# Scores and the K remainder of gate/up in 32-row TensorE tiles, two head groups alternating

## The chip, the cores and the metric

The kernel runs on one core of one Trainium2 chip. The metric is device time in microseconds (us), the median of the runs shown. TensorE does the matmuls, VectorE (DVE) and ScalarE (ACT) read their results from PSUM, GpSimd (POOL) masks, and SyncE (SP) issues most DMAs. All times here are in us unless marked ns.

## The reference

A transformer block with attention and a gated MLP side by side on the same normalized input. S = 2048 tokens, D = 576, 32 heads of 18, a causal window of 256 keys, F = 4608, all tensors bf16.

```python
xn  = layernorm(x)
q, k, v = split_heads(xn @ wqkv)                 # 32 heads x 18
p   = softmax(where(0 <= i - j < 256, q @ k.T * 18**-0.5, -1e9))
att = merge_heads(p @ v) @ wo
h   = silu(xn @ w1) * (xn @ w3)                  # 576 -> 4608
out = x + att + h @ w2                           # 4608 -> 576
```

## The kernel before

The program is a list of operations, each with its engine and the buffers it reads (`r`), writes (`w`) or writes further (`j`). From these `_Prog.resolve` works out the semaphore waits. Each engine runs its operations in the order of the list, so the order in the code is the schedule: an operation that waits holds up all that stands behind it on its engine.

The tokens are worked in four chunks of 512 (`c`), and each chunk has two stages.

The first stage loops over 36 units (`u`), each 128 columns of F. `unit_full` does up (`w3`) and gate (`w1`), four matmuls each with 128 rows of K. D = 576 leaves 64 rows, which `unit_rest` does as two matmuls on 64-row tiles of the array: one for up in rows 0 to 63, one for gate in rows 64 to 127. `unit_act` reads the up bank on VectorE (`us`, L541) and the gate bank on ScalarE (`th`, L543). `unit_h` makes `gs` (L549, which reads the gate bank again) and `hT` (L552) on VectorE.

Attention is laid between the units. A group `g` is four heads, a step `s` one key block of 128 against up to 384 queries; chunk 0 has three steps per group, later chunks four. Steps 1 and 2 have one part, steps 0 and 3 two parts of 128 and 256 columns. `scores` (L433) works on 64-row tiles, two heads to a tile with the other head's query rows zero, and writes four PSUM banks, the SBK banks. `exps` (L447) reads them in two pairs, `p` = 0 and 1. `masks` (L459) runs on GpSimd. Two units after a group's last step `pv` (L475) multiplies by v on four column tiles into the bank UB, `pv_out` copies it to `uT` (L484), and a unit later `heads_back` (L489) transposes it back and `heads_out` normalizes it into `oall`.

The next chunk's layer norm is also laid into the units: `ln_stats`, two units later `ln_apply` (L307), two later `xn_trans` (L317) through UB.

The second stage multiplies `hT` by W2 (`p2_item`, L584) and `oall` by `wo` into the SBK banks. Every eighth item it takes one tile of the next chunk's q, k or v projection (`qk_tile`, `v_half`) or, at four items, `o_trans`. `repack` (L385) moves q and k from `stage` into head layout by DMA, in chunk 0 on SP's queue, later on ScalarE's.

PSUM has eight banks: a ring of three (RB) for units and projections, four SBK, one UB. A unit takes two ring banks. In each iteration the order is

```python
unit_full(c, u); unit_rest(c, u)
scores(c, *step); pv(...); heads_back(...)
unit_act(u); exps(c, *step); unit_h(u)
pv_out(...); heads_out(...); masks(c, *step); ln_stats / ln_apply / xn_trans
```

The gate/up weights come in fills of 512 columns of F (`load_w13`, five DMAs each, three buffers), the remainder's weights among them (`wr`).

Of the kernel before, what the change touches and what calls it, by code (L numbers as in the profile page):

```python
# [162 lines left out]
def bass_parallel_sum__sliding_block__glu_gated_swiglu__prompt_kernel(  # L163
# [32 lines left out]
    with ExitStack() as es:  # L196
# [7 lines left out]
        xn = [sb(f"xn{i}", [128, D]) for i in range(2)]  # L204
# [5 lines left out]
        xnT = sb("xnT", [128, 2, 5, CH])  # L210
# [4 lines left out]
        wr = [sb(f"wr_{i}", [128, 512]) for i in range(NW13)]  # L215
# [3 lines left out]
        qk = sb("qk", [128, 4, G, CH])  # L219
        va = sb("va", [128, 2 * TB, G, 4 * VW])  # L220
        pt = sb("pt", [128, NPT, 2, 384])
        uT = [sb(f"uT{i}", [128, CH]) for i in range(2)]
# [9 lines left out]
        RB = es.enter_context(nc.psum_tensor("rb", [128, 3, 512], dt.float32))  # L232
        SBK = es.enter_context(nc.psum_tensor("sbk", [128, 4, 512], dt.float32))
        UB = es.enter_context(nc.psum_tensor("ub", [128, 512], dt.float32))
        UBH = UB[:, :].bitcast(dt.bfloat16)
        UT4 = UBH[:, 0:512].rearrange("p (t h c) -> p t h c", t=TB, h=4)

        ring_ctr = 0

        def ring():  # L240
            nonlocal ring_ctr
            i = ring_ctr % 3
            ring_ctr += 1
            return i

# [18 lines left out]
        def load_w13():  # L264
            nonlocal nfill
            if nfill >= NC * NFC:
                return
            s = nfill % NW13
            c0 = (nfill % NFC) * 512
            nfill += 1  # L270
            k = [("w13", s)]
            d = f"w13_{s}"
            add("sp", lambda e: e.dma_start(
                w3[s][:, 0:3, :], B_w3[0:384, c0:c0 + 512].rearrange("(kd p) f -> p kd f", p=128)), w=k, dma=d)
            add("sp", lambda e: e.dma_start(w3[s][:, 3, :], B_w3[448:576, c0:c0 + 512]), j=k, dma=d)
            add("sp", lambda e: e.dma_start(
                w1[s][:], B_w1[0:512, c0:c0 + 512].rearrange("(kd p) f -> p kd f", p=128)), j=k, dma=d)
            add("sp", lambda e: e.dma_start(wr[s][0:64, :], B_w3[384:448, c0:c0 + 512]), j=k, dma=d)
            add("sp", lambda e: e.dma_start(wr[s][64:128, :], B_w1[512:576, c0:c0 + 512]), j=k, dma=d)
# [25 lines left out]
        def ln_apply(t, s):  # L305
            i = t % 2
            add("dve", lambda e: e.tensor_scalar(  # L307
                xn[i][:], xp[s][:], mv[i][:, 0:1], rstd[i][:, 0:1], op0=ALU.subtract, op1=ALU.mult),
                r=[("xp", s), ("mv", i), ("rstd", i)], w=[("xn", i)])

        def xn_trans(t, bank, key, evac):
            i = t % 2
            c, tt = divmod(t, TB)
            bv = bank.rearrange("p (k f) -> p k f", f=128)
            for kd in range(5):
                k0 = min(kd * 128, D - 128)
                add("pe", lambda e, kd=kd, k0=k0: e.transpose(bv[:, kd, :], xn[i][:, k0:k0 + 128], ident[:]),  # L317
                    r=[("xn", i), "ident"], **{"w" if kd == 0 else "j": [key]})
            dst = xnT[:, c % 2, :, tt * 128:(tt + 1) * 128]
            if evac == "dve":  # L320
                add("dve", lambda e: e.tensor_copy(dst, bv[:, 0:5, :]), r=[key], w=[("xnT", c % 2, tt)])
            else:
                add("act", lambda e: e.activation(dst, bv[:, 0:5, :], ACT.Copy), r=[key], w=[("xnT", c % 2, tt)])
# [5 lines left out]
        def qk_tile(c, i):  # L329
# [6 lines left out]
            add("dve", lambda e: e.tensor_copy(stage[:, i, :], RB[:, b, :]), r=[("rb", b)], w=[("st", i)])  # L336
# [34 lines left out]
        def repack(c, g, eng):  # L371

            kq, kk = ("q", g), ("k", g, c % 2)
            first = True
            for hh in range(4):
                a, b = hh % 2, 2 + c % 2
                for tq, tk, rq, rk, o, n in pieces(Dh * (4 * g + hh)):
                    p0 = 32 * hh + o
                    if tq != tk:
                        moves = [(qk[p0:p0 + n, a:b + 1:b - a, g, :], stage[rq:rq + n, tq:tk + 1:tk - tq, :])]  # L380
                    else:
                        moves = [(qk[p0:p0 + n, a, g, :], stage[rq:rq + n, tq, :]),
                                 (qk[p0:p0 + n, b, g, :], stage[rk:rk + n, tk, :])]
                    for dst, src in moves:
                        add(eng, lambda e, dst=dst, src=src: e.dma_start(dst, src),  # L385
                            r=[("st", tq), ("st", tk)], dma=f"qk{g}", **{"w" if first else "j": [kq, kk]})
# [38 lines left out]
        def scores(c, g, s):  # L425
            for p in range(2):
                for r in range(2):
                    bk = 2 * p + r
                    first = True
                    for kb, qb, nq, col in parts(c, s):  # L430
                        kc, kt = divmod(kb, TB)
                        qo = (qb - c * TB) * 128
                        add("pe", lambda e, p=p, r=r, bk=bk, kc=kc, kt=kt, qo=qo, nq=nq, col=col: e.matmul(  # L433
                            SBK[:, bk, col:col + 128 * nq],
                            qk[64 * r:64 * r + 64, 2 + kc % 2, g, kt * 128:(kt + 1) * 128],
                            qk[64 * r:64 * r + 64, p, g, qo:qo + 128 * nq],
                            start=True, stop=True, tile_position=(64 * r, 0)),
                            r=[("k", g, kc % 2), ("q", g)], **{"w" if first else "j": [("sb", bk)]})
                        first = False

        def exps(c, g, s):
            nonlocal pt_ctr
            for p in range(2):
                sl = pt_ctr % NPT
# [3 lines left out]
                    pt[:, sl, :, :], SBK[:, 2 * p:2 * p + 2, 0:384], ACT.Exp, scale=scale),  # L448
                    r=[("sb", 2 * p), ("sb", 2 * p + 1)], w=[("pt", sl)])

        def masks(c, g, s):
            for p in range(2):
                sl = pt_of[(c, g, s, p)]
                v = pt[:, sl, :, :].rearrange("p h (b q) -> p h b q", q=128)
                key = [("pt", sl)]
# [10 lines left out]

        def pv(c, g):

            seq = [(s, part) for s in steps_of(c) for part in parts(c, s)]
            for n, (s, (kb, qb, nq, col)) in enumerate(seq):  # L470
                qo = (qb - c * TB) * 128
                for hh in range(4):
                    sl = pt_of[(c, g, s, hh % 2)]
                    slot = kb % (2 * TB)
                    add("pe", lambda e, hh=hh, sl=sl, slot=slot, qo=qo, nq=nq, col=col, n=n: e.matmul(  # L475
                        UB[32 * hh:32 * hh + VW, qo:qo + 128 * nq],
                        va[:, slot, g, VW * hh:VW * (hh + 1)],
                        pt[:, sl, hh // 2, col:col + 128 * nq],
                        start=(n == 0), stop=(n == len(seq) - 1), tile_position=(0, 32 * hh), skip_group_check=True),
                        r=[("pt", sl), ("va", slot)], **{"w" if n == 0 and hh == 0 else "j": ["ub"]})  # L480

        def pv_out(g):
            i = g % 2
            add("dve", lambda e: e.tensor_copy(uT[i][:], UB[:, :]), r=["ub"], w=[("uT", i)])  # L484

        def heads_back(g):
            i = g % 2
            for tt in range(TB):
                add("pe", lambda e, tt=tt: e.transpose(  # L489
                    UBH[:, tt * 128:(tt + 1) * 128], uT[i][:, tt * 128:(tt + 1) * 128], ident[:]),  # L490
                    r=[("uT", i), "ident"], **{"w" if tt == 0 else "j": ["ub"]})

        def heads_out(g):
            i = g % 2
            add("dve", lambda e: e.reciprocal(rden[i][:], UT4[:, :, :, Dh]), r=["ub"], w=[("rden", i)])
            ov = oall[:, :, g * 72:(g + 1) * 72].rearrange("p t (h d) -> p t h d", d=Dh)
            add("dve", lambda e: e.tensor_tensor(
                ov, UT4[:, :, :, 0:Dh], rden[i][:].unsqueeze(3).to_broadcast([128, TB, 4, Dh]), ALU.mult),
                r=["ub", ("rden", i)], w=[("o", g)])
# [16 lines left out]
        def unit_full(c, u):  # L516
            fc, fl = divmod(u, 4)
            sl = (c * NFC + fc) % NW13
            bu, bg = ring(), ring()
            unit_banks[u] = (bu, bg)  # L520
            for b, ws, blocks in ((bu, w3, (0, 1, 2, 4)), (bg, w1, (0, 1, 2, 3))):
                for kd in range(4):
                    add("pe", lambda e, kd=kd, b=b, ws=ws, xb=blocks[kd]: e.matmul(  # L523
                        RB[:, b, :], ws[sl][:, kd, fl * 128:(fl + 1) * 128], xnT[:, c % 2, xb, :],
                        start=(kd == 0), stop=False),
                        r=[("w13", sl)] + xk(c), **{"w" if kd == 0 else "j": [("rb", b)]})

        def unit_rest(c, u):
            fc, fl = divmod(u, 4)
            sl = (c * NFC + fc) % NW13  # L530
            bu, bg = unit_banks[u]
            for b, r, xb in ((bu, 0, 3), (bg, 1, 4)):
                add("pe", lambda e, b=b, r=r, xb=xb: e.matmul(  # L533
                    RB[:, b, :], wr[sl][64 * r:64 * r + 64, fl * 128:(fl + 1) * 128],
                    xnT[64 * r:64 * r + 64, c % 2, xb, :], start=False, stop=True, tile_position=(64 * r, 0)),
                    r=[("w13", sl)] + xk(c), j=[("rb", b)])
# [70 lines left out]
        def load_wa(key, d0, c0, n, first):  # L607
            k = {"w" if first else "j": [key]}
            add("sp", lambda e: e.dma_start(
                wa[:, 0:4, d0:d0 + n], A_wqkv[0:512, c0:c0 + n].rearrange("(kd p) f -> p kd f", p=128)), dma=key, **k)  # L610
            add("sp", lambda e: e.dma_start(wa[64:128, 4, d0:d0 + n], A_wqkv[512:576, c0:c0 + n]), j=[key], dma=key)

        load_wa("wv", 2 * D, 2 * D, D, True)
        load_wa("wqk", 0, 0, 512, True)
        load_wa("wqk", 512, D, 512, False)
        load_wa("wqk", 1024, 512, 64, False)
# [152 lines left out]
```

## Time and profile before

| what | value |
|---|---|
| median of 3 runs | 625.95 (625.16 to 626.57) |
| profiled execution, own time | 625.68 |
| its span | 624.0 |
| TensorE matmul busy | 612.3 (98%) |
| VectorE / ScalarE / GpSimd busy | 382.5 / 261.7 / 230.6 |
| first stage, chunk 0 / 1 / 2 / 3 | 95.2 / 97.3 / 97.3 / 96.0 |
| second stage, chunks 0 to 2 | 55.9 each |
| granted TensorE clock | 1.00 |

The stages' lengths are windows of the trace (26.3 to 121.5 is the first stage of chunk 0, and so on). A profile line gives start and length in time order (timeline), or busy time and mean length of a group (page). Matmuls are pipelined, so one line's length is not its cost; the distance between starts is. `[0.48 <-PE rb L533]` at a line's end is the idle time before it on its engine and what ended it.

### The profile page before, as it was taken

How to read it: one execution, taken by the hardware profiler on the slowest of the kernel's cores; microseconds unless marked ns; L12 is line 12 of the kernel's file. 1: busy time of each engine (PE TensorE's matmuls, PEld its weight loads, DVE VectorE, ACT ScalarE, POOL GpSimd, SP SyncE). 2: the span in 40 equal slices, each digit the busy share in tenths (PEclk: the TensorE clock that was granted, in tenths of full speed). 3: DMA queues.
4: the chain of work that ended last, by engine and by line, in shares of the span. 5: the costliest groups of instructions: out<-in, count | busy, mean ns of one | idle time of the engine just before them, and what ended most of it. 6: DMA issues, size and time to landing. Idle time of an engine off the chain costs nothing.

```text
span 624.0 us, 11857 instructions
## 1 busy us (share of the span) xinstructions
PE 612.3 (98%) x4788; PEld 329.3 (53%) x4788; DVE 382.5 (61%) x715; ACT 261.7 (42%) x397; POOL 230.6 (37%) x538
## 2 busy tenths in 40 slices
PE   5999999999999999999999999999999999999998
PEld 3434433367754444456774444445677444444776
DVE  5578889833048889873305888886330677777311
ACT  3276763200037677620005777771000677775000
POOL 6066673000026667610004666660000566664000
PEclk9999999999999999999999999999999999999999
DMA  8364546454534334354453425244445324330352
GB/s 238 106 187 151 176 115 192 147 150 121 148 88 140 109 99 140 115 157 132 105 160 93 137 86 159 80 149 146 132 119 151 104 79 130 99 115 1 91 140 74
DMA packets 101338, 78.92 MB, mean 126 GB/s; under 512 B 7844, under 2 KB 101284, under 8 KB 101284
## 3 DMA queue, kind: packets, MB, share of 16 engines
q1 hardware_dynamic: 96745, 74.64, 41.3%
q10 hardware_dynamic: 4539, 3.54, 2.0%
q8 instruction: 37, 0.61, 0.4%
q14 instruction: 17, 0.14, 0.1%
HBM read 71.07 MB, written 2.36 MB: 118 GB/s over the span
## 4 chain that ended last, share of the span: by engine, by line
PE 93%; DVE 3%; DMA 1%; SPq 1%; issue 0%
PE rb L523 39%; PE sbk L584 23%; PE rb L533 7%; PE rb L332 6%; PE sbk L433 6%; PE ub L475 4%; PE rb L343 4%; PE sbk L590 3%; PE ub L489 2%; DVE us L541 1%; DMA wa<-in_A_wqkv_dram 1%; DVE gs L549 1%; SPq L385 1%; PE ub L317 1%; PE rb L506 1%; DMA xp<-in_A_x_dram 0%
## 5 line engine op out<-in xcount | busy, mean ns | idle before, releaser
L459 POOL TENSOR_SCALAR_AFFINE_SELECT pt<-pt 128x256 bf16<-128x256 bf16 x480 | 209.2, 468 | 335.4 <-ACT pt L447 335.4
L523 PE MATMUL rb<-xnT,w 128*128 128x512 bf16 x1152 | 273.7, 380 | 1.2 <-DVE us L541 1.1
L543 ACT ACTIVATE th<-rb 128x512 bf16<-128x512 f32 x144 | 86.0, 597 | 308.8 <-PE rb L533 308.8
L447 ACT ACTIVATE pt<-sbk 128x768 bf16<-128x768 f32 x240 | 181.0, 812 | 0.0
L523 PEld LDWEIGHTS rb<-xnT,w 128*128 128x128 bf16 x1152 | 101.9, 98 | 123.2 <-issue 16.5
L584 PE MATMUL sbk<-w,hT 128*128 128x288 bf16 x1152 | 155.9, 286 | 0.0
L541 DVE TENSOR_SCALAR us<-rb 128x512 bf16<-128x512 f32 x144 | 98.8, 686 | 67.4 <-PE rb L533 67.0
L584 PEld LDWEIGHTS sbk<-w,hT 128*128 128x128 bf16 x1152 | 111.7, 98 | 33.4 <-issue 0.9
L549 DVE SCALAR_TENSOR_TENSOR gs<-th,rb 128x512 bf16<-128x512 bf16 x144 | 98.7, 685 | 0.0
L552 DVE TENSOR_TENSOR hT<-gs,us 128x512 bf16<-128x512 bf16 x144 | 64.2, 446 | 5.0
L597 DVE TENSOR_TENSOR ofin<-sbk,xp 128x288 bf16<-128x288 f32 x32 | 14.6, 456 | 80.4 <-PE sbk L590 80.3
L433 PE MATMUL sbk<-qk 64*128 64x256 bf16 (+2 forms) x704 | 58.9, 272 | 0.0
L533 PE MATMUL rb<-xnT,wr 64*128 64x512 bf16 x288 | 56.2, 387 | 0.0
L336 DVE CAST stage<-rb 128x512 bf16<-128x512 f32 x36 | 24.9, 692 | 44.1 <-PE rb L332 44.1
L533 PEld LDWEIGHTS rb<-xnT,wr 64*128 64x128 bf16 x288 | 13.8, 93 | 61.0 <-issue 61.0
L332 PE MATMUL rb<-xnT,wa 128*128 128x512 bf16 x180 | 43.4, 379 | 0.0
L433 PEld LDWEIGHTS sbk<-qk 64*128 64x128 bf16 x704 | 32.1, 95 | 14.8
L343 PE MATMUL rb<-wa,xnT 128*128 128x288 bf16 x160 | 26.3, 305 | 1.1 <-DMA wa<-in_A_wqkv_dram 1.1
L332 PEld LDWEIGHTS rb<-xnT,wa 128*128 128x128 bf16 x180 | 17.6, 98 | 16.0
L590 PE MATMUL sbk<-wo,oT 128*128 128x288 bf16 x160 | 25.8, 286 | 0.0
L475 PE MATMUL ub<-pt,va 128*20 128x256 bf16 (+2 forms) x704 | 25.4, 276 | 0.3
L354 DVE CAST va<-rb 128x288 bf16<-128x288 f32 x24 | 11.0, 457 | 20.7 <-PE rb L343 20.7
(40 smaller groups left out, 213.4 us busy)
## 6 DMA issues: line engine op xcount, KB each, us to landing
w<-in_B_w_dram SPq DMA_DIRECT2D x72, 288.0 KB, 3.2
w<-in_B_w_dram SPq DMA_DIRECT2D x36, 512.0 KB, 4.3
w<-in_B_w_dram SPq DMA_DIRECT2D x36, 384.0 KB, 3.3
xp<-in_A_x_dram SPq DMA_DIRECT2D x32, 144.0 KB, 3.8
w<-in_B_w_dram SPq DMA_DIRECT2D x36, 128.0 KB, 3.4
wr<-in_B_w_dram SPq DMA_DIRECT2D x72, 64.0 KB, 4.2
qk<-stage ACTq DMA_DIRECT2D x75, 36.0 KB
out_dram<-ofin SPq DMA_DIRECT2D x32, 72.0 KB, 1.7
```

Source lines behind the costliest of these rows:

```text
L332: add("pe", lambda e, kd=kd: e.matmul(RB[:, b, :], wa[:, kd, i * 128:(i + 1) * 128], xnT[:, c % 2, kd, :], start=(kd == 0), stop=(kd == 4) ...
L343: add("pe", lambda e, kd=kd: e.matmul(RB[:, b, 0:HD], xnT[:, c % 2, kd, tt * 128:(tt + 1) * 128], wa[:, kd, c0:c0 + HD], start=(kd == 0), ...
L433: add("pe", lambda e, p=p, r=r, bk=bk, kc=kc, kt=kt, qo=qo, nq=nq, col=col: e.matmul(SBK[:, bk, col:col + 128 * nq], qk[64 * r:64 * r + 64 ...
L447: add("act", lambda e, p=p, sl=sl: e.activation(pt[:, sl, :, :], SBK[:, 2 * p:2 * p + 2, 0:384], ACT.Exp, scale=scale), r=[("sb", 2 * p), ...
L459: add("pool", lambda e, vb=vb, edge=edge: e.affine_select(out=vb, in_=vb, compare_op=ALU.is_ge, fill=0.0, base=-1 if edge else 0, pattern= ...
L523: add("pe", lambda e, kd=kd, b=b, ws=ws, xb=blocks[kd]: e.matmul(RB[:, b, :], ws[sl][:, kd, fl * 128:(fl + 1) * 128], xnT[:, c % 2, xb, :] ...
L533: add("pe", lambda e, b=b, r=r, xb=xb: e.matmul(RB[:, b, :], wr[sl][64 * r:64 * r + 64, fl * 128:(fl + 1) * 128], xnT[64 * r:64 * r + 64, ...
L541: add("dve", lambda e: e.tensor_scalar(us[i][:], RB[:, bu, :], 0.5, None, op0=ALU.mult), r=[("rb", bu)], w=[("us", i)])
L543: add("act", lambda e: e.activation(th[i][:], RB[:, bg, :], ACT.Tanh, scale=0.5), r=[("rb", bg)], w=[("th", i)])
L549: add("dve", lambda e: e.scalar_tensor_tensor(out=gs[i][:], in0=th[i][:], scalar=1.0, in1=RB[:, bg, :], op0=ALU.add, op1=ALU.mult), r=[("t ...
L552: add("dve", lambda e: e.tensor_tensor(hT[:, u, :], gs[i][:], us[i][:], ALU.mult), r=[("gs", i), ("us", i)], w=[("h", u)])
L584: add("pe", lambda e: e.matmul(bank, hT[:, f, tt * 128:(tt + 1) * 128], w2[sl][:, k, :], start=(f == 0), stop=False), r=[("h", f), ("w2", ...
```

## The change

The remainder of K is cut into two pieces of 32 rows per matrix, so a unit has four remainder matmuls in place of two, on 32-row tiles: unit `u` uses rows 64*(u%2) to 64*(u%2)+63, up in the first 32, gate in the second. Scores use the other 64 rows: one head of 18 rows to a 32-row tile, without zero padding, odd groups in rows 64 to 127, even groups in rows 0 to 63. Two groups alternate unit by unit, so scores and remainder always have different rows. The order inside a unit with scores is that of `window_scores`, below. Units without scores are done in pairs: one unit's full matmuls, then both remainders, then the other unit's full matmuls (`pairs`). `xnT` gets a sixth block, which holds the last 64 rows in the orders that the row tiles need; `ln_apply` writes it in four instructions, `xn_trans` transposes six blocks.

PSUM becomes a ring of four and four SBK banks; `pv`, `heads_back` and `xn_trans` take a ring bank each. The remainder's weights stay resident (three parts of eight DMAs), a fill has two DMAs. The exp output gets six more slots inside `stage`. The GpSimd clears of `qk` go. The last groups' `pv` and `heads_back` fall into the second stage, and its projections begin after item 24.

```diff
         def ln_apply(t, s):
...
+            tail = xn[i][:, 512:768].rearrange("p (m a r d) -> p m a r d", m=2, r=2, d=32)
+            xtail = xp[s][:, 512:576].rearrange("p (a d) -> p a d", d=32).unsqueeze(2).to_broadcast([128, 2, 2, 32])
+            moves = ((xn[i][:, 0:512], xp[s][:, 0:512]), (tail[:, 0], xtail), (tail[:, 1, 0], xtail[:, 1]), (tail[:, 1, 1], xtail[:, 0]))
+            for n, (dst, src) in enumerate(moves):
...
-        def scores(c, g, s):
...
+        def score_mms(c, g, s, h):
+
+            r0 = 64 * (g % 2) + 32 * (h % 2)
+            gi = 2 * (g // 2) + h // 2
+            for n, (kb, qb, nq, col) in enumerate(parts(c, s)):
+                kc, kt = divmod(kb, TB)
+                qo = (qb - c * TB) * 128
+                add("pe", lambda e, kc=kc, kt=kt, qo=qo, nq=nq, col=col: e.matmul(
+                    SBK[:, h, col:col + 128 * nq],
+                    qk[r0:r0 + Dh, 1 + kc % 2, gi, kt * 128:(kt + 1) * 128],
+                    qk[r0:r0 + Dh, 0, gi, qo:qo + 128 * nq],
+                    start=True, stop=True, tile_position=(r0, 0)),
+                    r=[("k", g, kc % 2), ("q", g)], **{"j" if n else "w": [("sb", h)]})
+                yield
...
+        def unit_rest(c, u, ab, first=False):
+
+            for i, b in enumerate(unit_banks[u]):
+                r0 = 64 * (u % 2) + 32 * i
+                n0 = (u // 2) * 128
+                start = first and ab == 0
+                add("pe", lambda e, b=b, r0=r0, n0=n0, start=start: e.matmul(
+                    RB[:, b, :], wr[r0:r0 + 32, ab, n0:n0 + 128], xnT[r0:r0 + 32, c % 2, 4 + (ab + u) % 2, :],
+                    start=start, stop=(not first and ab == 1), tile_position=(r0, 0)),
+                    r=[wr_key(u)] + xk(c), **{"w" if start else "j": [("rb", b)]})
+
+        def window_scores(c, u, g, s):
+
+            rows = [score_mms(c, g, s, h) for h in range(4)]
+            unit_rest(c, u, 0)
+            for _ in zip(rows[0], rows[1]):
+                pass
+            next(rows[2])
+            next(rows[3])
+            unit_rest(c, u, 1)
+            for _ in zip(rows[2], rows[3]):
+                pass
+
+        def window_pair(c, u):
+
+            for ab in range(2):
+                unit_rest(c, u, ab)
+                unit_rest(c, u + 1, ab, first=True)
...
         for c in range(NC):
-            att = [(g, s) for g in range(G) for s in steps_of(c)]
-            at_unit = dict(enumerate(att))
-            per = len(steps_of(c))
-            pv_unit = {per * g + per - 1 + 2: g for g in range(G)}
+            att = [(2 * gp + 1 - n, s) for gp in range(G // 2) for s in steps_of(c) for n in range(2)]
+            pairs = {0, 2, 10, 18, 26, 34} if c == 0 else {0, 34}
+            alone = [u for u in range(NF) if u not in pairs and u - 1 not in pairs]
+            at_unit = dict(zip(alone, att, strict=True))
+            last = {g: u for u, (g, s) in at_unit.items()}
+            pv_unit = {}
+            for gp in range(G // 2):
+                u = last[2 * gp + 1] + 2
+                u += u in pairs
+                pv_unit[u] = 2 * gp + 1
+                pv_unit[u + 2] = 2 * gp
             fin_unit = {u + 1: g for u, g in pv_unit.items()}
             xt_unit = {}
             if c + 1 < NC:
-                xt_unit = {u: i for i, u in enumerate((9, 15, 21, 28) if c == 0 else (8, 16, 24, 28))}
+                xt_unit = {u: i for i, u in enumerate((14, 22, 25, 31) if c == 0 else (8, 16, 24, 32))}
...
-            ot_at = {20: 0, 44: 1, 68: 2, 92: 3}
+            ot_at = {44: 0, 60: 1, 76: 2, 92: 3}
             for n, item in enumerate(p2_list(c)):
                 p2_item(c, item, xs)
-                if n in ot_at:
+                u = NF + n // 8
+                if n % 8 == 3 and u in pv_unit:
+                    pv(c, pv_unit[u])
+                    pv_out(pv_unit[u])
+                elif n % 8 == 3 and u in fin_unit:
+                    heads_back(fin_unit[u])
+                    heads_out(fin_unit[u])
+                elif n in ot_at:
                     o_trans(ot_at[n])
```

## The prediction, made before the changed kernel ran

> **What bounds the kernel now.** I read the page first (busy time, slices, chain), then the timeline of single units, because one unit's rhythm repeats 144 times.
>
> ```profile
> PE 612.3 (98%) x4788; PEld 329.3 (53%) x4788; DVE 382.5 (61%) x715; ACT 261.7 (42%) x397; POOL 230.6 (37%) x538
> PE   5999999999999999999999999999999999999998
> PE 93%; DVE 3%; DMA 1%; SPq 1%; issue 0%
> ```
>
> TensorE is busy in every slice, and 93% of the chain is TensorE. But matmuls overlap, so a busy TensorE may still wait; starts tell more. The timeline of chunk 3, units 0 and 1:
>
> ```profile
> 483.83 1.89 PE L523 MATMUL rb<-xnT,w 128*128 128x512 bf16 x8
> ...
> 485.65 0.39 PE L533 MATMUL rb<-xnT,wr 64*128 64x512 bf16 x2
> ...
> 485.88 0.49 PE L433 MATMUL sbk<-qk 64*128 64x128 bf16 x8
> ...
> 486.11 0.60 ACT L543 ACTIVATE th<-rb 128x512 bf16<-128x512 f32 x1 [57.47 <-PE rb L533]
> ...
> 486.30 1.90 PE L523 MATMUL rb<-xnT,w 128*128 128x512 bf16 x8
> 486.60 1.51 ACT L447 ACTIVATE pt<-sbk 128x768 bf16<-128x768 f32 x2
> ...
> 488.14 0.39 PE L533 MATMUL rb<-xnT,wr 64*128 64x512 bf16 x2
> ...
> 488.36 0.49 PE L433 MATMUL sbk<-qk 64*128 64x384 bf16 x4
> ...
> 488.59 0.60 ACT L543 ACTIVATE th<-rb 128x512 bf16<-128x512 f32 x1 [0.48 <-PE rb L533]
> ...
> 488.78 0.39 PE L523 MATMUL rb<-xnT,w 128*128 128x512 bf16 x1
> ```
>
> Read starts. A unit with scores takes 2.48 (483.83 to 486.30, to 488.78). Its eight full matmuls start every 0.216. From the last of them to the first 64-row matmul (486.30+7x0.216=487.81 to 488.14) are 0.31: 0.10 more than a pitch, the price of a change of tile shape, paid again on the way back. The two 64-row matmuls lie side by side (0.39 for two of 0.387), as do the four 384-wide score matmuls by twos. From the 64-row start to the next full matmul it is 0.65; I call this the window. A unit without scores takes 2.15 (chunk 0, unit 30 to 31: 108.59 to 110.75). ACT is off the path: `th` starts 0.455 after the second 64-row matmul, the two exps end 2.00 after that (486.11 to 488.11), and the next `th` is ready later.
>
> VectorE and a late load show in the timeline of chunk 0:
>
> ```profile
> 44.95 0.46 DVE L297 BATCH_NORM_STATS2 stats<-xp 128x6 f32<-128x288 bf16 x1 [0.90 <-DMA xp<-in_A_x_dram]
> ...
> 45.93 0.64 DVE L541 TENSOR_SCALAR us<-rb 128x512 bf16<-128x512 f32 x1
> ...
> 46.63 1.04 PE L523 MATMUL rb<-xnT,w 128*128 128x512 bf16 x4 [1.08 <-DVE us L541]
> ...
> 48.02 0.69 DVE L541 TENSOR_SCALAR us<-rb 128x512 bf16<-128x512 f32 x1 [0.39 <-PE rb L533]
> ...
> 48.68 0.69 DVE L549 SCALAR_TENSOR_TENSOR gs<-th,rb 128x512 bf16<-128x512 bf16 x1
> ...
> 49.40 0.43 DVE L552 TENSOR_TENSOR hT<-gs,us 128x512 bf16<-128x512 bf16 x1
> ...
> 49.74 0.68 DVE L484 CAST uT<-ub 128x512 bf16<-128x512 f32 x1
> ```
>
> VectorE needs 1.72 a unit (48.02 to 49.74), 0.6 more for `uT`. TensorE resumes 0.06 after the copy it waited for (46.57 to 46.63). At the end of chunk 3's unit loop the timeline has
>
> ```profile
> 579.45 0.39 PE L533 MATMUL rb<-xnT,wr 64*128 64x512 bf16 x2
> ...
> 579.78 2.75 PE L584 MATMUL sbk<-w,hT 128*128 128x288 bf16 x21
> ```
>
> so W2's matmuls begin 0.33 after the last remainder and wait for nothing.
>
> **The change, part by part**, against the span of 624.0 (the profiled run is 625.68, the median 625.95; the median stands 1.95 above the span).
>
> *Scored windows, 120.* Each row tile pair now has 2x512 columns (remainder) or 2x384 (scores), all four abreast: 2x0.216 plus 0.10 for the way back, 0.53 in place of 0.65. Gain 120x0.12 = 14.4. That four run abreast no row shows for row tiles; pv's column tiles do it (four matmuls within 0.01 at 203.52). Ends: 0 lost, or two abreast only (a rival). I take four abreast.
>
> The Trainium skill, "TensorE: Matmul & The Clock Gate", Part 3, gives four row tiles of 512 a measured speedup of 3.07, not 4. By that each round would last 1.30 pitches, and an estimate of 0.13 a window would end the gain. The row of two abreast (0.39 against 0.387) shows no such loss, and I go by the row.
>
> *Pairs, 12.* Two units: 1.82 + 0.53 + 8x0.216 = 4.08 against 2x2.15 = 4.31. Gain 12x0.23 = 2.7.
>
> *The new order around the exps.* Scores 2 and 3 wait, as before, for the previous step's second exp. But now the second remainder round stands behind them on TensorE, and `th` waits for that round; full matmuls and everything else queue behind it too. So a loop closes within one unit: remainder to `th` 0.455, `th` to second exp's end 2.00, exp to TensorE 0.06, three starts 0.01: 2.53. Before, `th` needed only remainders ahead of the scores, and the same path had two units. Where nothing else lengthens a unit, it now takes 2.53, not 1.82+0.53 = 2.36. Between consecutive scored units with no pv, heads_back or xn transposes in between, I count 10 such steps in chunk 0, 15 in chunks 1 and 2, 19 in chunk 3: 59. Loss 59x0.17 = 10.0. Elsewhere pv (0.60 to 0.77 a group), heads_back (0.23) or transposes (0.34) cover the wait; without that cover each would cost 0.17 too.
>
> *End of the unit loop.* In every chunk the last odd group's pv is at unit 35 and its heads_back after W2 item 3. Its transposes wait for `uT`, which stands on VectorE behind units 34 and 35. From the last window's start: `us` of 34 at 0.64, of 35 at 2.37; `gs` of 35 waits for its `th` (2.50+0.60) to 3.13; `h` 3.85, `uT` 4.20 to 4.88, TensorE at 4.94. TensorE gets there at 2.36 (pv) + 0.77 + 4x0.1225 = 3.61, in chunk 0 at 3.44. Loss 3x1.33 + 1.49 = 5.5. The last pv at item 11 has eight items of cover before its heads_back (1.07 against 0.97 needed).
>
> *Extra changes of shape.* Seven pv groups follow a pair's second unit and four lie among W2 items, each with one change more: 11x0.10 = 1.1. The sixth transpose: 12x0.056 = 0.7, and 0.2 at the start, where the rest hides behind the v weights' landing (TensorE waits to 8.64).
>
> *VectorE and the ring of four.* `ln_apply` in four instructions: I bound it by 0.1 to 0.5 above the one of 0.57 to 0.63 (the smallest VectorE rows are 0.21 to 0.25 and overlap) and take 0.2. A bank taken by pv, heads_back or transposes shifts the ring, so the next unit's gate bank is the last unit's up bank, with 0.2 to 0.3 to spare. Chunks 1 and 2 stay inside that: the fullest unit needs 1.72+0.60+0.98 = 3.30 against 3.12. In chunk 0 statistics fall into pairs, and at units 14 and 22 heads_back and transposes together turn the ring by four banks, so the next unit waits for `us`. I get 0.5 at unit 12, 0.3 at 15, 0.5 at 20, 0.9 at 23: 2.2 (0 to 4).
>
> *Loads.* SP is busy without pause from 19.7 to 67 in chunk 0. Two DMAs a fill in place of five save 1.6 of its time each; remainder weights add eight per part. The x load of chunk 1 is then issued near 41 for statistics at unit 10 (near 50), so the wait of 0.90 and the three smaller ones go: gain 2.1. Remainder part 1 lands near 44, for unit 8 near 46: cover 2; without it unit 8 waits as long as it is late. The repacks still end on ACT's queue 10 or more before the next chunk.
>
> Sum: 14.4 + 2.7 + 2.1 = 19.2 gained; 10.0 + 5.5 + 1.1 + 0.9 + 2.2 = 19.7 lost. Span 624.5; median **626.4**.
>
> *Unlike lengths abreast.* No row has 512 beside 128 or 256, as steps 0 and 3 now do (56 windows). If a short matmul is only done with its longer neighbour, such a window lasts 0.11 more; about half are covered by the loop: 0 to 3.2. pv's tiles pass from 128 to 256 to 384 without a gap, so I take 0.
>
> The same page (Part 3, "The mechanism") says matmuls end strictly in program order. By that rule the 3.2 would be due; no run here shows it.
>
> **The rivals.** (1) *No change*, as summed: 33%. (2) *Slower, by windows longer than counted*: unlike lengths are held. It decides once the mean window is over about 0.55, price up to 3.2, plus 1 if VectorE's lag reaches chunks 1 and 2: 627.5 to 631. For it: no row of this shape. Against: equal lengths run abreast without loss. 37%. (3) *Faster*: VectorE keeps up in chunk 0 (2.2 back) and the loop closes in 2.50 (1.8 back): 622.5 to 624.7. For it: VectorE is only 61% busy. Against: the single steps above. 23%. (4) *Row tiles two abreast only*: 0.33 more on each of 120 windows, less the loop's 10.0 that it covers, plus 5 on the pairs: near 661, 4%. (5) *The exp loop does not bind*: 616, 3%; the exps' end at 2.00 is the same in all 120 rows, so I hardly believe it.
>
> **How the numbers follow.** About 0.2% (1.25 us) is what a measurement of this kernel can tell from no change. Faster is (3) and (5), 0.26; slower is (2) and (4), 0.41; same 0.33. The range leaves out (4) and (5) and the outer parts of (2) and (3): 622.5 to 631. The forecast's own range is 625.2 to 627.2.
>
> **What would show it.** Right: plain scored units of 2.52 to 2.53, with score matmuls released by ACT's exp; 3.1 with pv; a wait of 1.3 for `uT` before the first heads_back among W2's matmuls; pairs of 4.08; no wait for x in chunk 0. Wrong: plain units of 2.36 (no loop), windows over 0.55 where nothing is waited for (unlike lengths or fewer abreast), or waits for `us` or `gs` in chunks 1 to 3.

## The result and the profile after

The change made the kernel slower: 632.05 (631.79 to 632.72, 4 runs) against 625.56 for the kernel before in the same runs, a ratio of 1.0105 (95% interval 1.0086 to 1.0124). The forecast was 626.4 in a range of 622.5 to 631, so the time lies 1.05 above the range. The profiled run has a span of 630.1.

The page of the changed kernel, busy time, slices and chain:

```profile
PE 604.8 (96%) x5025; PEld 321.4 (51%) x5092; DVE 392.1 (62%) x762; ACT 262.2 (42%) x397; POOL 222.9 (35%) x521
PE   5999899999999999999999999999999999999998
PEclk9999799999999999999999999999999999999999
PE 89%; DVE 4%; SPq 3%; issue 2%; ACT 1%; DMA 1%; POOL 0%; ACTq 0%
```

Two things differ. SP's queue is on the chain with 3%, where it had 1%, and in the fifth slice (63 to 79) the granted clock reads 7 where it was 9: something in chunk 0 held TensorE, and its clock fell.

Cutting the span where a stage's first weight load stands gives the ledger. The predicted column puts the prediction's own terms into their stages (a pv and two heads_back move from each first stage to the second).

| stage | before | after | change | predicted |
|---|---|---|---|---|
| up to the first unit | 26.11 | 25.88 | -0.2 | +0.2 |
| first stage, chunk 0 | 95.41 | 99.38 | **+4.0** | **-3.0** |
| first stage, chunks 1 and 2, each | 97.39 | 94.52 | -2.9 | -2.7 |
| first stage, chunk 3 | 96.06 | 93.77 | -2.3 | -2.2 |
| second stage, each | 55.80 | 58.41 | +2.6 | +2.7 |

Eight of the nine stages went as forecast within 0.5. Chunk 0's first stage alone is 7.0 longer than forecast; the others together are some 1.4 shorter, so the span misses by 5.6 (630.1 against 624.5).

The timeline of chunk 3, plain units with scores, TensorE and ScalarE only:

```profile
497.92 0.39 PE L568 MATMUL rb<-xnT,wr 32*128 32x512 bf16 x2
...
498.29 0.39 PE L568 MATMUL rb<-xnT,wr 32*128 32x512 bf16 x2
...
498.61 1.90 PE L557 MATMUL rb<-xnT,w 128*128 128x512 bf16 x8
498.74 0.60 ACT L596 ACTIVATE th<-rb 128x512 bf16<-128x512 f32 x1 [0.52 <-PE rb L568]
499.24 1.51 ACT L474 ACTIVATE stage<-sbk 128x768 bf16<-128x768 f32 x2
...
500.44 0.39 PE L568 MATMUL rb<-xnT,wr 32*128 32x512 bf16 x2
500.45 0.69 PE L460 MATMUL sbk<-qk 18*128 18x384 bf16 x4
500.81 0.39 PE L568 MATMUL rb<-xnT,wr 32*128 32x512 bf16 x2
501.13 1.90 PE L557 MATMUL rb<-xnT,w 128*128 128x512 bf16 x8
```

From 498.61 to 501.13 a plain unit takes 2.52. The second remainder round starts 0.37 after the first (500.44 to 500.81), not 0.23: the exps end at 499.24+1.51=500.75, and 0.06 later TensorE goes on. That is the loop through ScalarE, at the size forecast.

Two windows where nothing waits, one with heads_back behind it, the other with pv, from the same trace:

```profile
518.84 0.39 PE L568 MATMUL rb<-xnT,wr 32*128 32x512 bf16 x2
518.85 0.39 PE L460 MATMUL sbk<-qk 18*128 18x128 bf16 x6
519.07 0.38 PE L568 MATMUL rb<-xnT,wr 32*128 32x512 bf16 x2
519.08 0.27 PE L460 MATMUL sbk<-qk 18*128 18x256 bf16 x2
519.38 0.40 PE L521 MATMUL rb<-ident,uT 128*128 128x128 bf16 x4
...
521.43 0.39 PE L568 MATMUL rb<-xnT,wr 32*128 32x512 bf16 x2
521.44 0.50 PE L460 MATMUL sbk<-qk 18*128 18x384 bf16 x4
521.66 0.38 PE L568 MATMUL rb<-xnT,wr 32*128 32x512 bf16 x2
521.97 0.34 PE L505 MATMUL rb<-stage,va 128*20 128x128 bf16 x8
```

Four row tiles do run abreast: score matmuls start 0.01 after the remainder's, the second round 0.23 after the first, and the next full-height work 0.54 after the start, against 0.53 forecast. The first window has score parts of 128 and 256 beside 512, the second parts of 384; in the windows of this trace whose second round is not held up, both kinds take the same 0.536 (medians of 22 and 39). So parts of unlike length hold nobody up.

The end of chunk 3's unit loop:

```profile
582.51 0.68 DVE L594 TENSOR_SCALAR us<-rb 128x512 bf16<-128x512 f32 x1
...
583.28 0.66 PE L637 MATMUL sbk<-w,hT 128*128 128x288 bf16 x4
...
584.32 0.68 DVE L514 CAST uT<-rb 128x512 bf16<-128x512 f32 x1
585.06 0.40 PE L521 MATMUL rb<-ident,uT 128*128 128x128 bf16 x4 [1.11 <-DVE uT L514]
```

After four W2 matmuls the next could start at 583.28+4x0.1225=583.77, but `uT` ends only at 585.00 and TensorE goes on at 585.06: a loss of 1.29 in chunk 3, forecast 1.33.

And the place that was not forecast, in chunk 0, ScalarE's timeline, SP's, and TensorE's:

```profile
62.68 0.60 ACT L596 ACTIVATE th<-rb 128x512 bf16<-128x512 f32 x1 [1.18 <-PE rb L568]
66.89 1.51 ACT L474 ACTIVATE stage<-sbk 128x768 bf16<-128x768 f32 x2 [3.61 <-DMA qk<-stage]
```
```profile
62.70 2.92 SPq L413 DMA_DIRECT2D qk<-stage  x4
65.66 0.47 SPq L786 DMA_DIRECT2D wo<-in_A_wo_dram  x1
```
```profile
65.35 0.39 PE L568 MATMUL rb<-xnT,wr 32*128 32x512 bf16 x2
67.75 0.50 PE L460 MATMUL sbk<-qk 18*128 18x384 bf16 x2 [2.01 <-ACT stage L474]
68.45 0.50 PE L460 MATMUL sbk<-qk 18*128 18x384 bf16 x2 [0.20 <-ACT stage L474]
...
69.00 1.03 PE L557 MATMUL rb<-xnT,w 128*128 128x512 bf16 x2
```

The exps of unit 14 write a slot inside `stage`. That slot is still to be read by the last group's repack, whose last DMA SP issues only at 64.9. So ScalarE waits 3.61, and with it the scores of unit 15 and the remainder behind them. Then the clock; windows of the same trace:

```profile
64.00:68.00 4.00, 1.99 (x11) 0.65 (x9) 1.57 (x5) 1.11 (x2) 0.24 (x1) 0.95 0.26 45
68.00:72.00 4.00, 3.80 (x14) 1.12 (x12) 1.77 (x3) 2.40 (x4) 2.75 (x8) 0.50 1.10 354
72.00:76.00 4.00, 4.00 (x32) 1.45 (x32) 1.77 (x3) 2.00 (x3) 1.26 (x4) 0.70 0.27 86
76.00:80.00 4.00, 3.84 (x34) 1.48 (x26) 3.01 (x5) 2.60 (x4) 2.48 (x7) 1.00 0.00 0
```

The column after the five engines is the granted clock: 0.50 while the matmuls catch up, with VectorE half idle. The score matmuls at 67.75 last 0.50 in place of 0.33.

### The profile page after: what moved, and what is told of

It is laid out like the page before. It is cut to its first block, busy times and chain, and to the rows that moved or that the text cites. A ratio compares the mean times of both kernels' runs of the same rounds, so it can differ in the third digit from the quotient of the medians.

```text
span 630.1 us, 12333 instructions
## 1 busy us (share of the span) xinstructions
PE 604.8 (96%) x5025; PEld 321.4 (51%) x5092; DVE 392.1 (62%) x762; ACT 262.2 (42%) x397; POOL 222.9 (35%) x521
## 4 chain that ended last, share of the span: by engine, by line
PE 89%; DVE 4%; SPq 3%; issue 2%; ACT 1%; DMA 1%; POOL 0%; ACTq 0%
PE rb L557 37%; PE sbk L637 22%; PE rb L568 6%; PE rb L358 6%; PE sbk L460 5%; PE rb L369 3%; PE sbk L643 3%; PE rb L505 3%; SPq L413 2%; PE rb L521 1%; DVE gs L602 1%; PE rb L343 1%; DVE xn L334 1%; DVE uT L514 1%; DVE hT L605 1%
## 5 line engine op out<-in xcount | busy, mean ns | idle before, releaser
L557 PE MATMUL rb<-xnT,w 128*128 128x512 bf16 x1095 | 264.9, 382 | 7.0 <-DVE us L594 3.4
L486 POOL TENSOR_SCALAR_AFFINE_SELECT pt<-pt 128x256 bf16<-128x256 bf16 x336 | 146.4, 468 | 238.6 <-ACT pt L474 238.6
L474 ACT ACTIVATE pt<-sbk 128x768 bf16<-128x768 f32 x168 | 126.7, 812 | 0.0
L486 POOL TENSOR_SCALAR_AFFINE_SELECT stage<-stage 128x256 bf16<-128x256 bf16 x144 | 62.1, 464 | 101.2 <-ACT stage L474 101.1
L568 PE MATMUL rb<-xnT,wr 32*128 32x512 bf16 x576 | 89.4, 384 | 0.1
L460 PE MATMUL sbk<-qk 18*128 18x384 bf16 (+2 forms) x704 | 70.6, 277 | 2.2 <-ACT stage L474 2.2
L474 ACT ACTIVATE stage<-sbk 128x768 bf16<-128x768 f32 x72 | 54.3, 812 | 3.6 <-DMA qk<-stage 3.6
L568 PEld LDWEIGHTS rb<-xnT,wr 32*128 32x128 bf16 x576 | 21.0, 91 | 56.5 <-issue 56.3
L358 PE MATMUL rb<-xnT,wa 128*128 128x512 bf16 x170 | 41.3, 379 | 0.5
L460 PEld LDWEIGHTS sbk<-qk 18*128 18x128 bf16 x704 | 24.1, 92 | 18.1 <-ACT pt L474 9.5
```

Source lines behind the costliest of these rows:

```text
L358: add("pe", lambda e, kd=kd: e.matmul(RB[:, b, :], wa[:, kd, i * 128:(i + 1) * 128], xnT[:, c % 2, kd, :], start=(kd == 0), stop=(kd == 4) ...
L460: add("pe", lambda e, kc=kc, kt=kt, qo=qo, nq=nq, col=col: e.matmul(SBK[:, h, col:col + 128 * nq], qk[r0:r0 + Dh, 1 + kc % 2, gi, kt * 128 ...
L474: add("act", lambda e, p=p, sl=sl: e.activation(pt_slot(sl), SBK[:, 2 * p:2 * p + 2, 0:384], ACT.Exp, scale=scale), r=[("sb", 2 * p), ("sb ...
L486: add("pool", lambda e, vb=vb, edge=edge: e.affine_select(out=vb, in_=vb, compare_op=ALU.is_ge, fill=0.0, base=-1 if edge else 0, pattern= ...
L557: add("pe", lambda e, kd=kd, b=b, ws=ws: e.matmul(RB[:, b, :], ws[sl][:, kd, fl * 128:(fl + 1) * 128], xnT[:, c % 2, kd, :], start=(first ...
L568: add("pe", lambda e, b=b, r0=r0, n0=n0, start=start: e.matmul(RB[:, b, :], wr[r0:r0 + 32, ab, n0:n0 + 128], xnT[r0:r0 + 32, c % 2, 4 + (a ...
```

## Experiments

The theory after the result: three separate places lose time, the slot in `stage` (chunk 0, with the clock), the loop through the exps, and the wait for `uT`. The rival: VectorE, with 79 busy of 95 in chunk 0 before, is the real limit, and the waits only cover it. The kernel before ran beside all these at 624.9 to 625.0.

**Slots outside `stage` in chunk 0.**

```diff
-                sl = pt_ctr % (NPT + NST)
+                sl = pt_ctr % (NPT + NST if c else NPT)
```

> Edit: in chunk 0 the exps use only the 14 slots of pt, not the six inside stage; the rest as in the changed kernel (632.05). Theory A: chunk 0 lost its time because the exps of unit 14 write a slot inside stage and wait until the last repack has read it (ACT waits 3.6 for the DMA, TensorE then 2.2, and its clock falls): without that the first stage of chunk 0 goes from 99.4 to 93.5 to 95, the mean granted clock to 1.00, the time to 626 to 628. Rival B: VectorE and the ring of four set chunk 0's length, as the prediction's 2.2 supposed, and the wait for the DMA only covers them: the gain is under 1.5, the time over 630.5.

Measured 626.53, ratio to the kernel before 1.0026 (1.0015 to 1.0037). Chunk 0's first stage is 94.01, the other stages are unchanged. ScalarE at the same place:

```profile
62.68 0.60 ACT L596 ACTIVATE th<-rb 128x512 bf16<-128x512 f32 x1 [1.18 <-PE rb L568]
63.17 1.51 ACT L474 ACTIVATE pt<-sbk 128x768 bf16<-128x768 f32 x2
```

and the windows of the same stretch:

```profile
64.00:68.00 4.00, 4.00 (x29) 1.39 (x27) 3.56 (x8) 2.66 (x4) 2.27 (x5) 1.00 0.31 64
68.00:72.00 4.00, 3.84 (x36) 1.55 (x32) 2.75 (x5) 2.97 (x6) 2.90 (x8) 1.00 1.09 338
```

Theory A holds. The slot cost 99.38-94.01 = 5.4. From unit starts, unit 15 shrinks from 5.48 to 2.37, unit 16 from 4.49 to 2.52, unit 17 from 2.81 to 2.52: 3.1 in the unit that waits, 2.3 in the two behind it, which ran at half clock.

**The third weight part behind the last repack**, slots left in `stage`.

```diff
-                if c == 0 and u == 9:
+                if c == 0 and u == 13:
                     load_wr(2)
```

> Edit: the changed kernel, but the third part of the remainder's weights is asked for at unit 13 of chunk 0, behind the last repack, in place of unit 9; the exp slots in stage stay. Theory A: the eight DMAs of that part (49.5 to 53.5 on SP) are what made the last repack late; it then ends near 61 instead of 65.6, before the exps of unit 14 want the slot at 63.2, so the whole wait and the fall of the clock go: as without the slots, chunk 0's first stage 94, time 626 to 627. Rival B: the slots in stage are too few anyway, or the loads behind are now late for unit 20: over 629.

Measured 626.22, 1.0023 (1.0011 to 1.0035); chunk 0's first stage 94.31, clock 1.00. SP's timeline:

```profile
55.34 7.28 SPq L413 DMA_DIRECT2D qk<-stage  x9
62.66 4.03 SPq L296 DMA_DIRECT2D wr<-in_B_w_dram  x8
```

The last repack is issued 3.0 earlier (at about 62 instead of 65), later than expected, and ScalarE still waits 1.0 for it:

```profile
63.89 1.51 ACT L474 ACTIVATE stage<-sbk 128x768 bf16<-128x768 f32 x2 [0.98 <-DMA qk<-stage]
```

Against the kernel without these slots that costs no more than 0.3. So the slots are enough; the order on SP's queue made them late. Two one-line edits, one at each end of the same wait, remove the same 5 us.

**heads_back later among W2's items.**

```diff
-                u = NF + n // 8
+                u = {3: 37, 19: 36, 27: 38}.get(n)
```

> Edit: among W2's items, the last even group's pv at item 3 and the two heads_back at items 19 and 27, in place of heads_back at 3, pv at 11, heads_back at 19. Theory A: TensorE's wait of 1.3 to 1.4 for uT at the first heads_back is real loss and goes away: each second stage 58.4 to 57.1, in all 5.3 less, 626.7. Rival B: VectorE is behind anyway, and the wait comes back at the new pv, at an output copy or at o_trans: less than 1 gained, over 631.

Measured 625.34, 1.0008 (0.9990 to 1.0025), better than expected. The second stages are 56.95, 57.12, 57.12 and 45.50 against 58.40, 58.41, 58.41 and 46.79: 5.3 less, as theory A says. VectorE's two `uT` copies now lie under other work:

```profile
577.41 0.68 DVE L594 TENSOR_SCALAR us<-rb 128x512 bf16<-128x512 f32 x1
...
579.22 1.28 DVE L514 CAST uT<-rb 128x512 bf16<-128x512 f32 x2
579.55 2.13 PE L637 MATMUL sbk<-w,hT 128*128 128x288 bf16 x16
581.52 0.39 PE L521 MATMUL rb<-ident,uT 128*128 128x128 bf16 x4
```

The further 1.3 is chunk 0 (98.11 in place of 99.38): the wait is there, but the clock came back sooner. In this trace the windows read

```profile
68.00:72.00 4.00, 3.64 (x14) 1.17 (x14) 1.78 (x3) 2.63 (x4) 2.75 (x7) 0.57 1.08 341
72.00:76.00 4.00, 3.84 (x37) 1.58 (x37) 2.40 (x4) 2.60 (x5) 2.23 (x6) 1.00 0.31 99
```

so half clock lasted about (1-0.57)x4/0.5 = 3.4, against (0.05+0.50+0.30)x4/0.5 = 6.8 in the changed kernel. The edit comes only after chunk 0's first stage, so it can't be its cause: the edit is worth the 5.3, the rest of the 6.7 is the clock. The ten executions of this kernel show the same. Three kept a mean granted clock of 1.00 (622.85 to 624.06), four had 0.997, the value of 3.4 at half clock (625.15 to 625.68), three 0.994 or 0.995, that of 6.8 (626.50 to 627.27). The changed kernel's four had 0.995 or 0.997; there the two with 0.997 were not the shorter ones, so single executions don't price the second stretch.

**Second remainder round ahead of scores 2 and 3.**

```diff
-            next(rows[2])
-            next(rows[3])
             unit_rest(c, u, 1)
```

> Edit: the second remainder round goes ahead of scores 2 and 3 in a scored window. Theory A: the loop of remainder, th, two exps, scores, remainder closes over two units instead of one: (2.06 + 0.455 + 0.22 + 0.16 + 0.10 + 1.83)/2 = 2.41, so plain scored units fall from 2.52 to 2.41, 59 of them, 6.5 less: 625.5. Rival B: the order is not the cause, ScalarE's own three instructions with their handovers set 2.52 a unit: no change, 631.5 to 632.5.

Measured 626.88, 1.0031 (1.0016 to 1.0046). Plain units alternate between 2.37 and 2.46, mean 2.415, as theory A said:

```profile
495.56 1.90 PE L557 MATMUL rb<-xnT,w 128*128 128x512 bf16 x8
...
497.93 1.90 PE L557 MATMUL rb<-xnT,w 128*128 128x512 bf16 x8
...
500.39 1.90 PE L557 MATMUL rb<-xnT,w 128*128 128x512 bf16 x7
```

Chunks 1 to 3 gain 1.4, 1.4 and 1.9. Chunk 0 does not (99.95): against the changed kernel ScalarE reaches the late slot 1.2 sooner (62.1) and the slot comes free 1.4 later (68.25), so the wait is 6.14 in place of 3.61. So 5.2 came, not 6.5.

**The three together.**

> Edit: the three edits together (14 slots in chunk 0, heads_back later, remainder first). Theory A: the three losses are independent places, so their gains add: 632.05 - 5 - 5.3 - 6.5 = 615.2, faster than the kernel before by about 10. Rival B: they share VectorE's time, which is near its limit once TensorE is faster (first stage of chunk 0: VectorE busy 79 of 95): under two thirds of the sum, over 621.

Measured 614.63, 0.9838 (0.9820 to 0.9856): 17.4 less than the changed kernel against 16.8 expected, so the three gains add, and the rival falls. In the traces chunk 0's first stage gives 6.3, the other first stages 4.8, the second stages 5.3, and an earlier first unit 0.6. First stages 93.06, 93.08, 93.08, 91.83, second stages as with the later heads_back, clock 1.00 throughout.

**Transposes of chunk 0 moved**, on top of the three: `xt_unit` (19, 23, 27, 31) for (14, 22, 25, 31).

> Edit: the three edits together, and the xn transposes of chunk 0 at units 19, 23, 27, 31 in place of 14, 22, 25, 31 (statistics and ln_apply four and two units ahead, as before). Theory A: at units 14 and 22 heads_back and transposes turn the ring of four by a whole turn while VectorE is late, so the next unit waits for us (4.48 at unit 22, 3.56 at 14, against 2.95 unhindered); apart from each other they cost less: chunk 0's first stage from 93.06 to 90.8 to 92, the three edits' 614.63 less 1 to 2.2. Rival B: VectorE's total in chunk 0 sets it, wherever the work lies: within 0.5.

Measured 614.47, 0.9837 (0.9819 to 0.9854): no gain that the time can tell. In the trace the first stage fell by 0.9 to 92.15, a little short of theory A's band and more than rival B allows. The waits at 14 and 22 are gone (2.55 each), but units 19, 20, 27 and 28 take longer instead (3.33, 2.98, 3.24, 2.98). The first unit began at 26.42 against 25.29, which hides the 0.9 in the span; over all these traces this start varies from 25.2 to 26.4. So the place of VectorE's work counts for 0.9, and most of the wait moves with the work: neither theory holds as it stands.

**The last two pv groups joined**, on top of that.

```diff
+            pv(c, pv_unit[37])
+            pv_out(pv_unit[37])
             proj = iter([])
...
-                u = {3: 37, 19: 36, 27: 38}.get(n)
+                u = {19: 36, 27: 38}.get(n)
```

> Edit: the same with the last two groups' pv straight behind each other at the end of the unit loop. Expected: two changes of tile shape less a chunk, 0.19, in four chunks 0.8 less than the kernel with the moved transposes. Rival: the second pv then waits for the last masks or for a ring bank, and nothing is gained.

Measured 613.10, 0.9817 (0.9797 to 0.9837), the fastest here, 11.9 below the kernel before. A chunk's two stages together fall from 93.08+57.12 to 93.74+56.25, 0.2 less in each of four chunks: the 0.8 expected. The rest of the 1.4 lies within the variation of the start. Chunk 0's first stage is 92.65 with one pv more, for which chunks 1 and 2 paid 0.66; without it it would be 91.99, so a second trace shows the fall of 0.9 or more from 93.06 by the moved transposes.

## Why the prediction was right and wrong

- **Window, pairs, changes of shape: right.** 0.536 for 0.53, pairs 4.11 in the traces (chunk 0: 2.58+1.53) for 4.08. The Trainium skill, "TensorE: Matmul & The Clock Gate", Part 3, gives four row tiles a speedup of 3.07; that is not seen here. The second round starts 0.226 after the first, where an estimate from the page's figure would make it 0.28. The strict order of ends that the same part states does not lengthen a window with unlike lengths either (0.536 both ways), so rival 2's mechanism is out; its band of times, 627.5 to 631, was nearly met by luck, for another cause.
- **The loop through the exps: right**, 2.52 for 2.53, and the re-ordering broke it to 2.415 as calculated.
- **The wait for `uT`: right**, 5.3 in all for 5.5.
- **Loads: this step failed.** It saw that SP is busy "from 19.7 to 67" in chunk 0, but of the repacks it asked only whether they end before the next chunk. The change lets the exps write into `stage`, so the end of a repack also releases a slot, and in chunk 0 such a slot is wanted at unit 14, near 63, while the last repack's last DMA is issued at 64.9. The added wait was put at nothing. It cost 5.4 of the 7.0, clock included.
- **VectorE in chunk 0: the term was mis-sized.** Without the slot, chunk 0's first stage was 94.0 where the terms make 92.4, so the 2.2 was rather 3.8. `ln_apply` in four instructions I took as 0.2 longer, at most 0.5. The kernel before, and the changed one:

```profile
50.34 0.63 DVE L307 TENSOR_SCALAR xn<-xp,mv,rstd 128x576 bf16<-128x576 bf16 x1
51.10 0.69 DVE L541 TENSOR_SCALAR us<-rb 128x512 bf16<-128x512 f32 x1
```
```profile
86.15 1.28 DVE L334 TENSOR_SCALAR xn<-xp,mv,rstd 128x512 bf16<-128x512 bf16 x4
87.34 0.68 DVE L594 TENSOR_SCALAR us<-rb 128x512 bf16<-128x512 f32 x1
```

Among the units of the changed kernel `us` follows the start of `ln_apply` 1.19 to 1.42 later; before, the one instruction lasted 0.63 at most. That is some 0.6 or more on top, outside my bound. Chunk 0 has four of them; at 0.4 each above what I took they would make 1.6, which is an estimate. A kernel with `ln_apply` in one instruction was not run, so the share of `ln_apply` in the 1.6 is argued, not shown. The slot's 5.4 and these 1.6, less the 1.4 that the other stages came out shorter, are the 5.6 by which the span missed.

## What to carry to other kernels

When buffers are shared, go through every new reuse and ask when its last reader is *issued*, on which queue and behind what, in each chunk and most of all in the first, where queues are fullest. In an engine that runs in order, draw each loop that passes through two engines and count how many units it spans: putting one matmul ahead of another opened such a loop from one unit to two. And a list of mechanisms that are right can still lack one: here eight stages of nine agreed within 0.5, and one overlooked wait made most of the difference.

## What the runs showed that I had not expected

- After a wait of TensorE of about 2.0 (65.74 to 67.75) the granted clock was half, for 6.8 in one trace and for 3.4 in another of the same place; three of the ten executions with the later heads_back kept the full clock. In the 3.4 before the fall (64.2 to 67.6) TensorE was still busy for 1.54. The Trainium skill, "TensorE: Matmul & The Clock Gate", Part 1, counts in windows of about 3.4 us and asks for an idle one; the lengths agree with one and two such windows, but the wait measured here is shorter than one.
- Waits of 1.3 for `uT` did not touch the clock.
- The four-instruction `ln_apply`: cutting 576 columns into pieces of 512, 128, 64 and 64, 768 in all, took 1.19 to 1.42 where the one instruction among the units lasted 0.63 at most.
